# Attention, routing and two expert layers on one core: constants, masks and one-hots of the routing laid out anew

## Chip, core and metric

The kernel runs on 1 core of one Trainium2 chip. The metric is device time in microseconds (us). The engines are named as in the profile: PE (TensorE, matrix products; PEld its weight loads), DVE (VectorE), ACT (ScalarE), POOL (GpSimd) and SP (SyncE, which issues DMAs).

## What is computed

A linear attention with a decaying state (4 batches, 8 heads, 768 steps, head size 48), then a mixture of 8 experts with the best two per token, then a gated layer:

```python
for t in range(S):                                   # per batch and head
    state = alpha[:, :, t, :, None] * state + k_t (outer) v_t
    y[:, :, t] = q_t @ state
x = y rearranged to [3072, 384]
noisy = x @ w_gate + log1p(exp(x @ w_noise)) * noise
top2 = the two largest of 8;  w = softmax over the two
out[token] += w * (relu(x[token] @ w1[e]) @ w2[e])    # e over the two experts
result = ((out @ w_a) * (out @ w_b)) @ w_out
```

## The kernel before

The 3072 tokens are 24 tiles of 128. The attention runs one loop over the tiles (lines 756 to 783), in chunks of 128 steps, with the heads in four pairs. The order of instructions is written out by hand, and every engine works through its own queue in that order. For tile i the loop emits, in this order: loads; transposes of k of tile i+1 (L643); transposes of the output of tile i-1 (L724); `inter(i)`, the product of q with the carried state (L667); `sc_unit(i+1)`, the scores q k of the next tile on PE (L651) and their causal mask on DVE (L656); `prep(i+3)`; `intra(i)` (L675), which uses the masked scores; `gm_unit(i-1)`, the gate products (L736); `u_unit` and `s_unit` (L702, L717, L718), the new state; and a piece of weight preparation (L110 on ACT, L111 on POOL) in tiles 6 to 21.

`prep` works out the decays. DVE scans backward (L621, "scan D") into `Ds` and forward (L625, "scan A") into `At`; POOL multiplies k by D (L623), q by A (L626), and makes the decay of the state (L629). Both scans take a reset pattern from `inject`, which fills PSUM bank 7: a 3-element memset (L620) sets the backward scan's ones, a reciprocal (L624) the values that the forward scan needs.

The scores of the even and the odd heads lie in PSUM banks 2 and 3; each is masked by an instruction of its own (L656, twice per tile) into `pm0` and `pm1`.

Routing runs beside this in pieces: generators in `side`, of which `tick()` advances each by one step. `choose(s)` (lines 236 to 309) works on a sub-group of 4 or 5 tiles (`SUBS`): logits and noise to the two best experts, with the softplus on ACT and POOL. `route(g)` (lines 311 to 404) follows for each of the two groups of 14 and 10 tiles (`GROUPS`): it counts ranks by products with triangular matrices, and makes the list of expert 0's tokens out of one-hot matrices (`eq`, `bt`, `at`, lines 365 to 378) whose products (L384) scatter token numbers into a table. `lists(g)` (lines 406 to 450) does the same for the other experts, in sets of 4 or 5 tiles (L426, L432, products L447). Gathers by these lists (L479) bring tokens together for the experts.

While POOL is busy, the small tiles of the first four sub-groups and of the first group lie in PSUM bank 5 (`place`, lines 177 to 187), those of the last ones in SBUF. Bank 6 (`UG`) holds the state products (L702), the gate products and the list tables. Accesses of two engines to one bank are ordered one after the other.

The one-hot tiles are 16-bit with the position innermost (`[tile, 128]` or `[tile, 49]`); `lane` and `keys`, the constants that they are compared with, are 16-bit too, the values compared (`pf`, `kf`, `val`, `token`) are 32-bit and constant along the innermost axis.

From 152 us on PE runs the experts' products (L801 to L803) and, from about 580 us, the gated layer's.

Of the kernel before, what the change touches and what calls it, by code (L numbers as in the profile page):

```python
# [7 lines left out]
F32 = mybir.dt.float32  # L8
F32R = mybir.dt.float32r
F16 = mybir.dt.float16  # L10
# [9 lines left out]
NP = H // 2  # L20
# [3 lines left out]
E = 8  # L24
# [33 lines left out]
def moe_kernel(ctx: ExitStack, tc, qka, afirst, v, wgn, noise, w1, w2, w3, out):  # L58
# [10 lines left out]

    def bank(i):  # L70
        return tl(psum, [128, 512], F32, f"bank{i}")
# [131 lines left out]
    def route_consts():  # L203
        nc.sync.dma_start(wgn_t, wgn)
        nc.sync.dma_start(noise_t, noise)
        iota(e4096, [[4096, E]])
        iota(prio, [[-1, E]], base=E)
        iota(keys.rearrange("p (e j) -> p e j", e=E), [[32, E], [1, NJ]])
        iota(lane, [[1, 128]])
        iota(token, [[256, NT // 2], [1, 2]], base=-1024, channel=2)  # L210
# [25 lines left out]
    def choose(s):  # L236
# [10 lines left out]
        def scr(name, *shape):  # L247
            return scratch(name, (5, *shape), last)[:, :n]
# [7 lines left out]
        lg = scr("lg", E)  # L256
        z, az, ex, w, c, r, ln, mz, sp = (tmp(x) for x in ("z", "az", "ex", "w", "c", "r", "ln", "mz", "sp"))
# [53 lines left out]
    def route(g):  # L311
# [34 lines left out]
        pi, ki = (scr(x, I32) for x in ("pi", "ki"))  # L346
        pf, kf, val = (scr(x) for x in ("pf", "kf", "val"))
        ri = val.bitcast(I32)
# [12 lines left out]
        else:  # L361
# [3 lines left out]
        eq, bt = (tl(rt, [128, HOT, 2, WL], F16, x, bufs=2).rearrange("p a k w -> p (a k w)")[:, :n * NJ]  # L365
                  .rearrange("p (a w) -> p a w", a=n) for x in ("eqk", "bt"))
        nc.vector.tensor_tensor(val, oav[:, :, 0], token[:, i0:i0 + n], op=ALU.mult)
        nc.vector.tensor_tensor(eq, keys[:, None, :NJ].to_broadcast([128, n, NJ]),
                                kf[:, :, None].to_broadcast([128, n, NJ]), op=ALU.is_equal)
        nc.vector.tensor_tensor(bt, eq, val[:, :, None].to_broadcast([128, n, NJ]), op=ALU.mult)  # L370
        yield
        m = n if n <= 2 * HOT else n // 2
        ats = []
        for j0 in range(0, n, m):
            at = tl(rt, [128, HOT, 2, 128], F16, "at", bufs=2).rearrange("p a k w -> p (a k) w")[:, :m]
            nc.vector.tensor_tensor(at, lane[:, None, :].to_broadcast([128, m, 128]),
                                    pf[:, j0:j0 + m, None].to_broadcast([128, m, 128]), op=ALU.is_equal)
            ats.append(at)
            yield
# [3 lines left out]
        for j in range(n):  # L383
            nc.tensor.matmul(pl, ats[j // m][:, j % m], bt[:, j], start=j == 0, stop=j == n - 1)  # L384
# [20 lines left out]

    def lists(g):
# [4 lines left out]
                          for x, dt in (("ei", I32), ("ri", I32), ("rf", F32), ("e1", F32)))  # L411
# [7 lines left out]
        def make(s):  # L419
            j0, j1 = s  # L420
            m = j1 - j0
            at, eq, bt = (tl(rt, [128, HOT, 2, w_], F16, x, bufs=2)[:, :m]
                          for x, w_ in (("at", 128), ("eqk", WL), ("bt", WL)))
            for out_, src, val in ((at, lane, pf), (eq, keys[:, NJ:], kf)):
                w_ = src.shape[-1]
                nc.vector.tensor_tensor(out_.rearrange("p a k w -> p (a k) w"),  # L426
                                        src[:, None, :].to_broadcast([128, 2 * m, w_]),
                                        val[:, j0 - i0:j1 - i0].rearrange("p a k -> p (a k)")[:, :, None]
                                        .to_broadcast([128, 2 * m, w_]), op=ALU.is_equal)
                yield  # L430
            for k in range(2):
                nc.vector.tensor_tensor(bt[:, :, k], eq[:, :, k],  # L432
                                        token[:, j0:j1, None].to_broadcast([128, m, WL]), op=ALU.mult)
            hot[s] = m, at, bt

        yield from make(sets[0])
        for s, after in zip(sets, sets[1:] + [None]):
            if after:
                yield from make(after)
            else:  # L440
                for _ in range(LAG - 1):
                    yield
            m, at, bt = hot.pop(s)
            pl = spot(1, WL)
            for j in range(m):
                for k in range(2):
                    nc.tensor.matmul(pl, at[:, j, k], bt[:, j, k], start=j + k == 0, stop=j == m - 1 and k == 1)  # L447
            yield
            nc.vector.tensor_tensor((idx if s[1] == NT else lacc)[:, NJ:], pl, lacc[:, NJ:], op=ALU.add)
        yield  # L450

    def weights():

        ei, ri, rf = (tl(rt, [128, NT, 2], dt, x) for x, dt in (("ei", I32), ("ri", I32), ("rf", F32)))
# [114 lines left out]
    with ExitStack() as actx:  # L569
        big = actx.enter_context(tc.tile_pool(name="abig", bufs=1))  # L570
        work = actx.enter_context(tc.tile_pool(name="awork", bufs=2))
# [27 lines left out]
        nc.vector.memset(inject, 0.0)  # L599
        Ds = [tl(big, [128, 512], F32, f"D{i}") for i in range(2)]  # L600
# [12 lines left out]
        def prep(i):  # L613
# [6 lines left out]
            nc.vector.memset(inject[:, 128::128], 1.0)  # L620
            nc.vector.tensor_tensor_scan(Dt[:, :511][:, ::-1], t[:, 1025:1536][:, ::-1], inject[:, 1:][:, ::-1], 1.0,  # L621
# [25 lines left out]
        def sc_unit(i):  # L647
            pb = [bank(2), bank(3)]
            for p in range(NP):
                for h in range(2):  # L650
                    nc.tensor.matmul(pb[h][:, p * 128:p * 128 + 128], part(i, h, NP + p), part(i, h, p),  # L651
                                     start=True, stop=True)
            PM[i] = []
# [102 lines left out]
        for i in range(NT):  # L756
# [9 lines left out]
            if i + 1 < NT:  # L766
                sc_unit(i + 1)
            else:
                x_unit(0, 0, bank(2))
                x_unit(0, 1, bank(3))  # L770
# [19 lines left out]

    hpool = sctx.enter_context(tc.tile_pool(name="hpool", bufs=1))
# [490 lines left out]
```

## Time and profile before

| | |
|---|---|
| time, median of 3 runs | 1036.9 us (1036.23 to 1038.09) |
| profiled execution: its time | 1040.05 us |
| profiled execution: its span | 1038.30 us |
| mean granted TensorE clock | 0.982 |
| busy: PE, DVE, ACT, POOL | 1005.3, 563.1, 385.1, 414.6 us |

All times in the rows below count from the start of the span of the profiled execution. A row of the timeline gives start, duration, engine, line, operation, output and inputs, and in brackets how long the engine stood idle before it and what released it; "x2" is two instructions merged in one row. Rows of one line give the shortest, the median and the longest duration of its instructions in ns. L656 is line 656 of the kernel before. "bank" is a PSUM bank; other names are SBUF tiles unless the text says otherwise.

### The profile page before, as it was taken

The page shows a single profiled execution, that of the slowest core. Times are in us where ns is not written, and L with a number is a line of the kernel's source. Part 1 is how long each engine was busy: PE and PEld are TensorE (multiplying, and loading weights), DVE is VectorE, ACT ScalarE, POOL GpSimd, SP SyncE. Part 2 cuts the span into 40 slices and gives each one's busy share as a digit, 9 for nine tenths or more (in the row PEclk, how much of TensorE's full clock was granted, in tenths as well). Part 3 has the DMA queues.
Part 4 walks back from the last instruction along what each step waited for, and adds up shares of the span by engine and source line. Part 5 has one row for each costly group of instructions (what it writes and reads, how often), then busy time and mean ns, then how long its engine had stood idle before and what let it go on. Part 6 is the DMA issues. An engine that isn't in the chain of part 4 may idle for free.

```text
span 1038.3 us, 17572 instructions
## 1 busy us (share of the span) xinstructions
PE 1005.3 (97%) x6698; PEld 931.8 (90%) x6698; DVE 563.1 (54%) x983; ACT 385.1 (37%) x831; POOL 414.6 (40%) x443
## 2 busy tenths in 40 slices
PE   7999689999999999999999999999999999999997
PEld 5888679999999999999999888888888888888886
DVE  8998667576676776767764454232233332333221
ACT  2555331454444444545443344222222222222212
POOL 5687441475766676868673334020020020000000
PEclk9999679999999999999999999999999999999999
DMA  9787110657686886897856535131140140020000
GB/s 334 263 300 244 59 55 27 182 177 215 210 236 188 233 239 197 236 249 222 221 156 182 143 107 137 38 104 18 42 111 1 46 107 1 31 62 1 31 1 33
DMA packets 118850, 141.13 MB, mean 136 GB/s; under 512 B 66272, under 2 KB 102752, under 8 KB 118752
## 3 DMA queue, kind: packets, MB, share of 16 engines
q1 hardware_dynamic: 112224, 120.13, 38.6%
q0 software_dynamic: 6528, 19.67, 6.6%
q8 instruction: 64, 1.05, 0.4%
q14 instruction: 34, 0.28, 0.1%
HBM read 101.43 MB, written 38.34 MB: 135 GB/s over the span
## 4 chain that ended last, share of the span: by engine, by line
PE 79%; DVE 7%; issue 3%; DMA 2%; POOL 2%; ACT 1%; SPq 0%; POOLq 0%; DVEq 0%
PE bank L801 25%; PE bank L803 25%; PE bank L802 25%; DVE pm L656 1%; DVE D L621 1%; DVE A L625 1%; DMA row<-xd,idx 1%; POOL W L111 1%; PE bank L667 1%; PE bank L651 1%; DMA xt<-tb 1%; PE bank L487 0%; DMA raw<-xt 0%; DMA y<-o 0%; POOL row L479 0%
## 5 line engine op out<-in xcount | busy, mean ns | idle before, releaser
L1113 DVE TENSOR_TENSOR p<-bank,a 128x512 f32<-128x512 f32 x72 | 49.8, 691 | 253.2 <-PE bank L803 253.2
L111 POOL TENSOR_TENSOR W<-wst,W 128x384 fp32r<-128x384 f32 x136 | 147.9, 1097 | 88.7 <-ACT W L110 83.5
L801 PE MATMUL bank<-X,W 128*128 128x416 f32 (+4 forms) x474 | 168.6, 356 | 0.5 <-ACT X L489 0.4
L802 PE MATMUL bank<-X,W 128*128 128x416 f32 (+3 forms) x474 | 167.8, 354 | 0.0
L803 PE MATMUL bank<-X,W 128*128 128x416 f32 (+3 forms) x474 | 167.7, 354 | 0.0
L801 PE MATMUL bank<-HB,W 128*128 128x416 f32 (+4 forms) x474 | 167.5, 353 | 0.0
L803 PE MATMUL bank<-HB,W 128*128 128x416 f32 (+3 forms) x474 | 166.5, 351 | 0.0
L802 PE MATMUL bank<-HB,W 128*128 128x416 f32 (+3 forms) x474 | 166.5, 351 | 0.0
L975 POOL DMA_INDIRECT row<-y,row x48 | 47.0, 978 | 206.0 <-DVE row L983 170.4
L845 ACT ACTIVATE HB<-bank 128x416 fp32r<-128x416 f32 (+2 forms) x128 | 65.9, 517 | 109.7 <-PE bank L803 96.4
L1111 ACT ACTIVATE a<-bank 128x512 f32<-128x512 f32 x72 | 43.1, 599 | 167.9 <-PE bank L803 166.0
L1115 ACT ACTIVATE HB<-p 128x512 fp32r<-128x512 f32 x72 | 45.5, 632 | 156.8 <-DVE p L1113 152.5
L846 DVE SCALAR_TENSOR_TENSOR HB<-bank,HB 128x416 fp32r<-128x416 f32 (+2 forms) x128 | 72.7, 582 | 45.4 <-ACT HB L845 41.1
L801 PEld LDWEIGHTS bank<-X,W 128*128 128x128 f32 x474 | 89.7, 189 | 4.6 <-ACT X L489 0.6
L803 PEld LDWEIGHTS bank<-X,W 128*128 128x128 f32 x474 | 89.6, 189 | 4.1
L802 PEld LDWEIGHTS bank<-X,W 128*128 128x128 f32 x474 | 89.7, 189 | 3.6
L803 PEld LDWEIGHTS bank<-HB,W 128*128 128x128 f32 x474 | 89.0, 188 | 4.0
L801 PEld LDWEIGHTS bank<-HB,W 128*128 128x128 f32 x474 | 89.1, 188 | 3.6
L802 PEld LDWEIGHTS bank<-HB,W 128*128 128x128 f32 x474 | 89.0, 188 | 3.7
L1116 DVE TENSOR_TENSOR HB<-p,HB 128x512 fp32r<-128x512 f32 x72 | 49.8, 692 | 50.3 <-ACT HB L1115 50.3
L110 ACT ACTIVATE W<-wst 128x384 fp32r<-128x384 f32 x144 | 71.9, 515 | 10.3 <-DMA wst<-w 8.6
L479 POOL DMA_INDIRECT row<-xd,idx x56 | 58.9, 1052 | 39.8 <-DVE idx L388 23.1
(240 smaller groups left out, 1960.9 us busy)
## 6 DMA issues: line engine op xcount, KB each, us to landing
wst<-w SPq DMA_DIRECT2D x128, 192.0 KB
ring<-qka SPq DMA_DIRECT2D x22, 768.0 KB
wd<-w SPq DMA_DIRECT2D x36, 384.0 KB
y<-o SPq DMA_DIRECT2D x56, 156.0 KB
xt<-tb SPq DMA_DIRECT2D x11, 768.0 KB
raw<-xt SPq DMA_DIRECT2D x44, 192.0 KB
w3f<-u SPq DMA_DIRECT2D x36, 192.0 KB
wst<-w3f SPq DMA_DIRECT2D x36, 192.0 KB
```

What stands on the lines that cost most here:

```text
L110: nc.scalar.activation(h, raw, AF.Copy)
L111: eng.tensor_tensor(l, raw, h.bitcast(F32), op=ALU.subtract)
L479: nc.gpsimd.indirect_dma_start(out=t[:m], out_offset=None, in_=xd[:SPLIT * 128] if a else xd, in_offset=bass.IndirectOffsetOnAxis(ap=ix, a ...
L801: nc.tensor.matmul(ps[:, :m], ah, bh[:, :m], start=first, stop=False)
L802: nc.tensor.matmul(ps[:, :n], ah, bl[:, :n], start=False, stop=False)
L803: nc.tensor.matmul(ps[:, :n], al, bh[:, :n], start=False, stop=last)
L845: nc.scalar.activation(Hh[:, f, s], pu[:, :n], AF.Relu)
L846: nc.vector.scalar_tensor_tensor(Hl[:, f, s], pu[:, :n], 0.0, Hh[:, f, s].bitcast(F32), op0=ALU.max, op1=ALU.subtract)
L975: nc.gpsimd.indirect_dma_start(out=t, out_offset=None, in_=src, in_offset=bass.IndirectOffsetOnAxis(ap=row[:, i, k:k + 1], axis=0))
L1113: nc.vector.tensor_tensor(p, ps[1], a, op=ALU.mult)
L1115: nc.scalar.activation(h, p, AF.Copy)
L1116: nc.vector.tensor_tensor(l, p, h.bitcast(F32), op=ALU.subtract)
```

## The change

- The backward scan gets a constant `resets` in SBUF, written once by POOL; the memset of each tile goes. The forward scan keeps `inject` in PSUM.
- The two score banks become one tile of two banks, and one instruction of 1024 elements per partition masks both.
- `lg` of `choose`, the logits without noise, always lies in SBUF.
- `pf`, `kf`, `val` and `token` become 16-bit and lie in SBUF. The one-hot tiles are turned: the position is the outer axis, the tiles of a set are innermost, so that every operand runs along the innermost axis. `lane` and `keys` are written out ten times over for that. `bt` of a set is one instruction instead of two. PE reads each one-hot at a stride of the number of tiles in it.
- Tiles of `weights` get names of their own.

```diff
-    keys = tl(rt, [128, E * NJ], F16, "keys")
-    lane = tl(rt, [128, 128], F16, "lane")
-    token = tl(rt, [128, NT], F32, "token")
+    keys = tl(rt, [128, E * NJ, 2 * HOT], F16, "keys")
+    lane = tl(rt, [128, 128, 2 * HOT], F16, "lane")
+    token = tl(rt, [128, NT, 2], F16, "token")
...
-        lg = scr("lg", E)
-        z, az, ex, w, c, r, ln, mz, sp = (tmp(x) for x in ("z", "az", "ex", "w", "c", "r", "ln", "mz", "sp"))
+        z, az, ex, w, c, r, ln, mz, sp, lg = (tmp(x) for x in ("z", "az", "ex", "w", "c", "r", "ln", "mz", "sp", "lg"))
...
-        pi, ki = (scr(x, I32) for x in ("pi", "ki"))
-        pf, kf, val = (scr(x) for x in ("pf", "kf", "val"))
-        ri = val.bitcast(I32)
+        pi, ki, ri = (scr(x, I32) for x in ("pi", "ki", "ri"))
+        pf, kf, val = (tmp(x, 1, F16) for x in ("pf", "kf", "val"))
...
+            at = hot_tile("at", 128, m)
+            nc.vector.tensor_tensor(at, lane[:, :, :m], pf[:, None, j0:j0 + m].to_broadcast([128, 128, m]),
+                                    op=ALU.is_equal)
...
-            nc.tensor.matmul(pl, ats[j // m][:, j % m], bt[:, j], start=j == 0, stop=j == n - 1)
+            nc.tensor.matmul(pl, ats[j // m][:, :, j % m], bts[j // m][:, :, j % m], start=j == 0, stop=j == n - 1)
...
+    def hot_tile(name, w, m):
+
+        size = {"at": 128, "eqk": WL, "bt": WL}[name]
+        t = tl(rt, [128, size * 2 * HOT], F16, name, bufs=2)
+        return t[:, :w * m].rearrange("p (w t) -> p w t", t=m)
...
-            for k in range(2):
-                nc.vector.tensor_tensor(bt[:, :, k], eq[:, :, k],
-                                        token[:, j0:j1, None].to_broadcast([128, m, WL]), op=ALU.mult)
+            nc.vector.tensor_tensor(bt, eq, token[:, j0:j1].rearrange("p a k -> p (a k)")[:, None, :]
+                                    .to_broadcast([128, WL, 2 * m]), op=ALU.mult)
...
+        resets = tl(big, [128, 512], F32, "resets")
+        nc.gpsimd.memset(resets, 0.0)
+        nc.gpsimd.memset(resets[:, ::128], 1.0)
...
-            nc.vector.memset(inject[:, 128::128], 1.0)
-            nc.vector.tensor_tensor_scan(Dt[:, :511][:, ::-1], t[:, 1025:1536][:, ::-1], inject[:, 1:][:, ::-1], 1.0,
+            nc.vector.tensor_tensor_scan(Dt[:, :511][:, ::-1], t[:, 1025:1536][:, ::-1], resets[:, 1:][:, ::-1], 1.0,
                                          op0=ALU.mult, op1=ALU.add)
...
-            pb = [bank(2), bank(3)]
+            pb = scores()
...
-            for h in range(2):
-                m = tl(work, [128, NP, 128], F32, f"pm{h}")
-                nc.vector.tensor_tensor(m, pb[h].rearrange("p (a t) -> p a t", a=NP),
-                                        causal[:, None, :].to_broadcast([128, NP, 128]), op=ALU.mult)
-                PM[i].append(m)
+            m = tl(work, [128, 2, NP, 128], F32, "pm")
+            nc.vector.tensor_tensor(m.rearrange("p h a t -> p (h a) t"), pb.rearrange("p h (a t) -> p (h a) t", a=NP),
+                                    causal[:, None, :].to_broadcast([128, 2 * NP, 128]), op=ALU.mult)
```

## Rows read from the trace of the kernel before

**Rows 1.** The page's chain that ended last, by engine, shares of the span.

```profile
PE 79%; DVE 7%; issue 3%; DMA 2%; POOL 2%; ACT 1%; SPq 0%; POOLq 0%; DVEq 0%
```

**Rows 2.** Stretches: length, busy us (instructions) of PE, PEld, DVE, ACT, POOL; clock, DMA.

```profile
52.00:84.00 32.00, 29.95 (x583) 27.41 (x582) 29.99 (x71) 16.87 (x45) 28.29 (x38) 1.00 0.82 291
84.00:107.00 23.00, 20.88 (x363) 19.07 (x363) 19.36 (x43) 12.46 (x35) 17.70 (x25) 0.93 0.69 246
186.00:1038.00 852.00, 843.56 (x4353) 786.12 (x4352) 415.22 (x645) 312.82 (x642) 309.65 (x293) 1.00 0.45 126
```

**Rows 3.** Timeline, DVE: the mask of a tile without routing work.

```profile
29.55 1.29 DVE L656 TENSOR_TENSOR pm<-bank,causal 128x512 f32<-128x512 f32 x2 [0.32 <-PE bank L651]
```

**Rows 4.** Timeline, DVE and POOL: a tile with a part of `choose`.

```profile
48.91 0.51 POOL L718 TENSOR_TENSOR sc<-ss,aend 128x192 f32<-128x192 f32 x1
...
49.39 1.22 DVE L621 TENSOR_TENSOR_SCAN D<-ring,bank 128x511 f32<-128x511 f32 x1
...
50.29 1.00 POOL L111 TENSOR_TENSOR W<-wst,W 128x384 fp32r<-128x384 f32 x1
...
51.60 0.27 POOL L280 TENSOR_TENSOR r_sp<-r_sp,noise 128x40 f32<-128x40 f32 x1
51.83 1.27 POOL L623 TENSOR_TENSOR ring<-ring,D 128x512 f32<-128x512 f32 x1
...
52.00 0.18 DVE L284 TENSOR_TENSOR bank<-r_sp,bank 128x40 f32<-128x40 f32 x1
...
53.42 1.28 DVE L656 TENSOR_TENSOR pm<-bank,causal 128x512 f32<-128x512 f32 x2
...
54.80 1.22 DVE L621 TENSOR_TENSOR_SCAN D<-ring,bank 128x511 f32<-128x511 f32 x1
```

**Rows 5.** One-hots and the nearest faster DVE line (ns); timeline: `bt`, and who waits.

```profile
L426 DVE TENSOR_TENSOR at<-lane,rf x5: 1214/1486/1493, 143.7 to 175.7; 128x1280 f16<-128x1280 f16 x4, 128x1024 f16<-128x1024 f16 x1
...
L942 DVE TENSOR_SCALAR u<-wd x36: 340/350/1656, 196.1 to 534.7; 128x384 int32<-128x384 int32 x36
...
147.12 0.72 DVE L432 TENSOR_TENSOR bt<-eqk,token 128x245 f16<-128x245 f16 x2
...
151.32 0.83 PE L736 MATMUL bank<-wgn,gx 128*64 128x16 f32 x12 [2.27 <-DVE lacc L449]
```

**Rows 6.** Lines (ns: shortest, median, longest) and timeline: DVE and POOL on SBUF together.

```profile
L952 DVE SCALAR_TENSOR_TENSOR u<-wd,rf x36: 501/1360/1883, 201.4 to 544.1; 128x384 int32<-128x384 int32 x36
...
222.85 1.61 DVE L952 SCALAR_TENSOR_TENSOR u<-wd,rf 128x384 int32<-128x384 int32 x1
223.00 1.03 POOL L111 TENSOR_TENSOR W<-wst,W 128x384 fp32r<-128x384 f32 x1
...
145.46 0.66 DVE L426 TENSOR_TENSOR eqk<-keys,e 128x490 f16<-128x490 f16 x1
145.62 0.63 POOL L306 TENSOR_TENSOR oa<-oh,oh 128x40 f32<-128x40 f32 x1 [3.38 <-DVE oh L298]
...
L626 POOL TENSOR_TENSOR ring<-ring,A x23: 1263/1276/1289, 11.0 to 131.8; 128x512 f32<-128x512 f32 x23
```

**Rows 7.** The same stretches for line L621 (scan D) alone: busy us (instructions).

```profile
52.00:84.00 32.00, 7.31 (x6) 1.00 0.82 291
84.00:107.00 23.00, 5.18 (x5) 0.93 0.69 246
```

**Rows 8.** Timeline, ACT and PE: sub-group 3's logits beside the first group's routing.

```profile
122.00 0.19 ACT L259 ACTIVATE bank<-bank 128x40 f32<-128x40 f32 x1 [3.26 <-DVE bt L370]
...
122.24 0.88 PE L702 MATMUL bank<-v,kn 128*48 128x48 f32 x16 [4.30 <-ACT bank L259]
```

**Rows 9.** Timeline, PE's weight loads: strided, contiguous, and of one-hots as they are.

```profile
148.10 0.42 PEld L487 LDWEIGHTS bank<-ident,row 128*128 128x128 f32 x3
...
148.44 0.37 PEld L724 LDWEIGHTS bank<-ident,x 128*128 128x128 f32 x3
...
154.17 0.51 PEld L447 LDWEIGHTS <-at 128*128 128x128 f16 x10 [0.31 <-issue]
```

More of the change, by code (lines that the diff above doesn't have):

```diff
@@ L68, in moe_kernel @@
     psum = ctx.enter_context(tc.tile_pool(name="psum", bufs=1, space=PSUM))
+    late = []
     def bank(i):
-        return tl(psum, [128, 512], F32, f"bank{i}")
+        return tl(late[0] if i in (2, 3) else psum, [128, 512], F32, f"bank{i}")
     xd = tc.dram_tile([N, DM], F32, name="xd")
@@ L207, in route_consts @@
         iota(prio, [[-1, E]], base=E)
-        iota(keys.rearrange("p (e j) -> p e j", e=E), [[32, E], [1, NJ]])
-        iota(lane, [[1, 128]])
-        iota(token, [[256, NT // 2], [1, 2]], base=-1024, channel=2)
+        iota(keys.rearrange("p (e j) t -> p e j t", e=E), [[32, E], [1, NJ], [0, 2 * HOT]])
+        iota(lane, [[1, 128], [0, 2 * HOT]])
+        iota(token, [[256, NT // 2], [1, 2], [0, 2]], base=-1024, channel=2)
         nc.gpsimd.memset(lacc, 1024.0)
@@ L364, in route @@
         yield
[L365 to L370, printed above, removed]
+        m = n if n <= 2 * HOT else n // 2
+        nc.vector.tensor_tensor(val, oav[:, :, 0], token[:, i0:i0 + n, 0], op=ALU.mult)
+        bts, ats = [], []
+        for j0 in range(0, n, m):
+            eq, bt = (hot_tile(x, NJ, m) for x in ("eqk", "bt"))
+            nc.vector.tensor_tensor(eq, keys[:, :NJ, :m], kf[:, None, j0:j0 + m].to_broadcast([128, NJ, m]),
+                                    op=ALU.is_equal)
+            nc.vector.tensor_tensor(bt, eq, val[:, None, j0:j0 + m].to_broadcast([128, NJ, m]), op=ALU.mult)
+            bts.append(bt)
         yield
-        m = n if n <= 2 * HOT else n // 2
-        ats = []
         for j0 in range(0, n, m):
-            at = tl(rt, [128, HOT, 2, 128], F16, "at", bufs=2).rearrange("p a k w -> p (a k) w")[:, :m]
-            nc.vector.tensor_tensor(at, lane[:, None, :].to_broadcast([128, m, 128]),
-                                    pf[:, j0:j0 + m, None].to_broadcast([128, m, 128]), op=ALU.is_equal)
+            at = hot_tile("at", 128, m)
+            nc.vector.tensor_tensor(at, lane[:, :, :m], pf[:, None, j0:j0 + m].to_broadcast([128, 128, m]),
+                                    op=ALU.is_equal)
             ats.append(at)
@@ L421, in make @@
             m = j1 - j0
-            at, eq, bt = (tl(rt, [128, HOT, 2, w_], F16, x, bufs=2)[:, :m]
-                          for x, w_ in (("at", 128), ("eqk", WL), ("bt", WL)))
+            at, eq, bt = (hot_tile(x, w_, 2 * m) for x, w_ in (("at", 128), ("eqk", WL), ("bt", WL)))
             for out_, src, val in ((at, lane, pf), (eq, keys[:, NJ:], kf)):
[L425 to L429, printed above, removed]
+                w_ = src.shape[1]
+                nc.vector.tensor_tensor(out_, src[:, :, :2 * m],
+                                        val[:, j0 - i0:j1 - i0].rearrange("p a k -> p (a k)")[:, None, :]
+                                        .to_broadcast([128, w_, 2 * m]), op=ALU.is_equal)
                 yield
-            for k in range(2):
-                nc.vector.tensor_tensor(bt[:, :, k], eq[:, :, k],
-                                        token[:, j0:j1, None].to_broadcast([128, m, WL]), op=ALU.mult)
+            nc.vector.tensor_tensor(bt, eq, token[:, j0:j1].rearrange("p a k -> p (a k)")[:, None, :]
+                                    .to_broadcast([128, WL, 2 * m]), op=ALU.mult)
             hot[s] = m, at, bt
@@ L446, in lists @@
                 for k in range(2):
-                    nc.tensor.matmul(pl, at[:, j, k], bt[:, j, k], start=j + k == 0, stop=j == m - 1 and k == 1)
+                    nc.tensor.matmul(pl, at[:, :, 2 * j + k], bt[:, :, 2 * j + k], start=j + k == 0,
+                                     stop=j == m - 1 and k == 1)
             yield
@@ L570, in moe_kernel, with scores @@
         big = actx.enter_context(tc.tile_pool(name="abig", bufs=1))
+        pss = actx.enter_context(tc.tile_pool(name="pss", bufs=1, space=PSUM))
+        def scores():
+            return tl(pss, [128, 2, 512], F32, "scores")
         work = actx.enter_context(tc.tile_pool(name="awork", bufs=2))
@@ L768, in moe_kernel @@
             else:
-                x_unit(0, 0, bank(2))
-                x_unit(0, 1, bank(3))
+                pb = scores()
+                x_unit(0, 0, pb[:, 0])
+                x_unit(0, 1, pb[:, 1])
             if i + 3 < NT:
@@ L788, in moe_kernel @@
         tick()
+    late.append(ctx.enter_context(tc.tile_pool(name="psum2", bufs=1, space=PSUM)))
     hpool = sctx.enter_context(tc.tile_pool(name="hpool", bufs=1))
```

8 lines of the change are left out of this document (4 added, 4 removed).

## Prediction, made before the changed kernel was run

> **What bounds the kernel now.** First the chain that ended last: 79% of it is PE [rows 1]. Then the table of stretches [rows 2]: from 186 us to the end PE is busy 843.56 of 852.00 us at a mean granted clock of 1.00, in products that the change doesn't touch, so whatever is won or lost before that should reach the end unchanged. The question is the attention stage. In 52 to 84 us PE has 29.95 of 32.00, DVE 29.99 and POOL 28.29 busy: three engines, none with much room. The timeline says who waits for whom. In the quiet tiles around 30 us DVE's mask waits 0.32 us for PE's scores [rows 3]: there PE sets the pace. From about 49 us on, when POOL also splits weights (L111) and does a part of `choose`, DVE goes from the mask to scan D without a gap [rows 4].
>
> **Part 1, resets in SBUF, one mask.** Removed: the 3-element memset and one of two masks per tile. A mask pair takes 1.28 us [rows 4]. The two lengths of the one-hot row give the price of an element, (1486 - 1214) / 256 = 1.06 ns, and a fixed part of 1486 - 1280 x 1.0625 = 126 ns [rows 5]; one mask of 1024 elements is then 1.21 us, 0.07 less. From the end of the mask (53.42 + 1.28 = 54.70) to scan D are 0.10 us [rows 4]; nearly all of that is the memset. So 0.15 us of DVE time a tile, 3.6 us over 24 if DVE set every pace. From 24 to 49 us it doesn't [rows 3]; there the saving only lengthens the wait for PE. I take -0.4 us, for the first three tiles (ends 0 and -3.6). Added: POOL writes `resets` and ten times larger `keys` and `lane`, at the very start, while its first work for the tiles comes later; nothing.
>
> Moved: scan D's second operand from PSUM to SBUF, so that scan D has two SBUF inputs. What that means is seen away from the scan. L952 has two SBUF inputs; it takes 0.50 us at its shortest, 1.36 in the median, 1.88 at most. At 222.85 it takes 1.61 us, and ends (224.46) after POOL's L111 (to 224.03) with about the length that it needs alone. The other way round POOL's L306 takes 0.63 us for 40 elements (L718, with 192, needs 0.51 [rows 4]) while DVE makes `eqk` (to 146.12) from two SBUF inputs: it ends at 146.25. Beside the scans as they are, with one operand in PSUM, POOL's L626 never varies: 1263 to 1289 ns over 23 [rows 6]. So a DVE instruction with two SBUF inputs and a POOL instruction exclude each other here, whole instruction by whole instruction. No row shows it for a scan.
>
> The Trainium skill has this as a rule (SBUF — State Buffer, Who interferes with whom): a Vector instruction with two SBUF inputs contends with a GpSimd instruction that reads SBUF, and whoever is first blocks the other for the whole instruction. By it, scan D joins in; by the rows alone a scan could still be an exception. The page measures no scan.
>
> What it costs, from both sides. Floor: in 52 to 84 us POOL's 28.29 plus six scans, 7.31 [rows 7], are 35.6 us for a stretch of 32.0: +3.6. In 84 to 107, 17.70 + 5.18 = 22.9 of 23.0: 0. Ceiling: each of the eleven scans costs its whole 1.22: +13.4. Between them, by walking the tile at 49 us [rows 4]. DVE asks for scan D 0.15 early, at 49.25; POOL's L718 holds until 49.42; D runs to 50.64. All that POOL does next (`choose`'s products, L111, to L280 at 51.60 + 0.27) moves by 1.22 us and ends at 53.1. L623 follows it at once, as it does now (51.83), until 54.3. Behind L280 DVE waits with L284; with `lg` in SBUF this too has two SBUF inputs, and comes after L623: 54.3 instead of 52.00. DVE's queue is in order, so the rest of `choose` and the mask (53.42) move by 2.3 us. The next scan D then meets L111 again: L623 to 54.3, L626 1.28, L718 0.51, L111 1.00, so not before 57.1 against 54.80. With a further wait of some 0.2 us in the second tile of the pair that is +2.5 us for one `choose`. Three lie between 49 and 107 us (sub-groups 0 to 2): +7.5 us. I take that, since the walk follows the queues; plain tiles I leave at nothing, as DVE has some slack there.
>
> **Part 2, logits in SBUF.** `lg` of sub-group 3 now lies in PSUM bank 5, where DVE works on `route(0)`: ACT's L259 waits 3.26 us, until L370 is done, and PE's L702, which needs bank 6 free of ACT, waits 4.30 us for L259 [rows 8]. With `lg` in SBUF, L259 runs at 122.00 - 3.26 = 118.74, L702 at about 119.0, and PE's next scores come as much earlier. Next late is DVE, with `route(0)`'s one-hots; they end before those scores. -3.1 us (ends -3.3, and 0 if another wait takes its place).
>
> **Part 3, one-hots.** Now 1280 elements take 1.49 us, `eqk` 0.66, the two halves of `bt` 0.72 together [rows 5, 6]. Afterwards all operands are 16-bit and run along the innermost axis. No row shows a two-operand DVE instruction above one element per 1.06 ns; the nearest faster one is L942, one operand, 384 in 350 ns: (350 - 126) / 384 = 0.58 ns an element [rows 5]. At that rate 1280 take 0.87, `eqk` and an undivided `bt` 0.41 each: 2.87 becomes 1.69, 1.2 us per set. Unchanged rate: about 0.1. I take the faster one. On the path lie the two sets before L736, which waits 2.27 us for L449 behind them [rows 5]. Of 2.4 us I count -1.5, since in front of L449 DVE also has to finish X of the third tile, which waits for ACT (ends 0 and -2.27). Later sets run beside PE's products: 0.
>
> The Trainium skill (VectorE: DVE Perf Modes, the perf-mode tier table) gives `tensor_tensor` on 16-bit SBUF operands twice the rate, and no more. An estimate by it, 1280 x 1.06 / 2 + 126 = 0.80 us, would make this term hardly different; no run yet shows it.
>
> PE now reads the one-hots at a stride of up to 10 elements. The trace has a strided load, every third column of `row` (L487), three in 0.42 us, against 0.37 for contiguous `x` (L724): 17 ns more each [rows 9]. 58 products after 141 us, where PE is the bound: +1.0 us. Ends: 0, and 58 times the difference between 0.37 / 3 = 123 and 51 ns (ten present loads in 0.51, L447): +4.2. Pool and bank naming, the split `ei`, `ri`, `rf`: nothing, as no wait names them.
>
> **Sum.** -0.4 + 7.5 - 3.1 - 1.5 + 1.0 = +3.5 us. The profiled execution took 1040.05 us (span 1038.30) and would take 1043.55; it stands 3.15 over the median, so the forecast is 1036.9 + 3.5 = 1040.4 us.
>
> **Rivals.** A, faster: scan D doesn't exclude POOL. Then the ten tiles of 52 to 107 us in which DVE sets the pace win 0.15 each: -0.4 - 1.5 - 3.1 - 1.5 + 1.0 = -5.5, 1031.4 us. For it: no row has such a scan, and the scan takes over 2 ns an element (1.22 us for 511), so it needn't read in every cycle. Against: [rows 6]. It decides if POOL's L111 keeps running under scan D.
> B, no change: they exclude each other, but POOL's lag is taken up by the three tiles that `prep` is ahead, and only the floor is left: -0.4 + 3.6 - 3.1 - 1.5 + 1.0 = -0.4, 1036.5 us. Against: L718 stands behind the lag in POOL's queue, and ACT, then PE, wait for it within a tile.
> C, slower still: PE's longer waits lower its clock. In 84 to 107 us the mean grant is 0.93 [rows 2]; of the two levels, 1.2 and 2.4 GHz, that is 14% or 3.2 us at the lower one, 1.6 us of work lost. Once more per `choose`: +4.8, 1045.2 us.
> That the change doesn't do what it says, one-hots at the old rate, gives 1041.9, inside the forecast's range.
>
> **How the numbers follow.** Forecast 0.40, A 0.27, B 0.23, C 0.10. About 0.2%, 2.1 us, is what a measurement can tell from no change. Faster: A and 0.04 of B, 0.31. Same: 0.15 of B and 0.09 of the forecast's low side, 0.24. Slower: the rest, 0.45. The range from 1030.5 to 1045.5 takes in A and most of C and leaves out the tails of both; the forecast's own is 1037.5 to 1043.5.
>
> **What would show it.** In the changed profile: scan D longer than 1.22 us in many of its 24, or POOL's L111, L718 and `choose` products stretched under it; L284 waiting behind L623; tile periods from 49 to 107 us up by some 0.7 on the mean; no wait of L259 on L370 and none of L702 over 1.5 us near 119 us; the 1280-element one-hot near 0.8 to 0.9 us; strided loads a little longer. POOL and scan D unmoved beside each other would overturn the main term and give A.

## The result, and the profile after

The changed kernel takes 1049.8 us in the median against 1036.9 before: ratio 1.0111, 95% interval 1.0077 to 1.0145. Two later groups of executions of the same kernel gave 1.0085 (1.0066 to 1.0104) and 1.0077 (1.0064 to 1.0091). It is slower, as forecast, but by 11.5, 8.8 and 8.0 us by these ratios (12.9 by the two medians of the first group) where 3.5 were forecast. The profiled execution took 1051.33 us (span 1049.6). In what follows a ratio is turned into us with the median of before that was timed beside it; a thousandth is 1.04 us.

The page's chain that ended last, by engine, answers to [rows 1]; the stretches (length, busy us and instructions of PE, PEld, DVE, ACT, POOL; clock, DMA) answer to [rows 2]. The stretch from 20 to 36 us is added; its line for the kernel before stands at the end.

```profile
PE 87%; DVE 6%; POOL 2%; issue 2%; DMA 1%; ACT 1%; SPq 0%; POOLq 0%; DVEq 0%; ACTq 0%
```

```profile
20.00:36.00 16.00, 14.14 (x236) 13.05 (x230) 10.38 (x14) 4.99 (x12) 9.60 (x12) 0.79 0.51 177
52.00:84.00 32.00, 28.65 (x506) 26.07 (x502) 25.34 (x41) 14.35 (x39) 27.43 (x36) 0.89 0.68 239
...
84.00:107.00 23.00, 21.05 (x289) 19.80 (x286) 17.28 (x32) 11.40 (x32) 17.64 (x21) 0.73 0.58 211
...
186.00:1038.00 852.00, 850.08 (x4402) 792.09 (x4401) 414.87 (x652) 311.61 (x641) 311.59 (x296) 1.00 0.44 126
```

```profile
20.00:36.00 16.00, 15.18 (x290) 14.14 (x291) 14.42 (x26) 7.12 (x17) 11.15 (x14) 1.00 0.74 261
```

Up to 107 us PE is nearly as busy as before but does less: 236 instructions in 20 to 36 instead of 290, at a mean granted clock of 0.79 instead of 1.00, and 289 in 84 to 107 instead of 363, at 0.73 instead of 0.93. The timeline of all engines at 22 us shows how that begins; the second fence has the same steps of the kernel before.

```profile
21.91 1.21 DVE L633 TENSOR_TENSOR_SCAN D<-ring,resets 128x511 f32<-128x511 f32 x1
21.93 1.19 POOL L641 TENSOR_TENSOR aend<-af,D 128x4 f32<-128x4 f32 x1
...
23.08 0.50 POOL L728 TENSOR_TENSOR sc<-ss,aend 128x192 f32<-128x192 f32 x1
...
23.61 0.73 ACT L701 ACTIVATE Sbd<-sc 64x192 f32<-64x192 f32 x2 [2.37 <-POOL sc L728]
...
24.40 1.13 PE L677 MATMUL bank<-Sbd,ring 128*128 128x96 f32 x8 [1.60 <-ACT Sbd L701]
...
26.70 1.95 PE L685 MATMUL bank<-v,pm 128*64 128x48 f32 x32
```

```profile
21.16 0.20 POOL L629 TENSOR_TENSOR aend<-af,D 128x4 f32<-128x4 f32 x1
...
22.65 1.13 PE L667 MATMUL bank<-Sbd,ring 128*128 128x96 f32 x8 [0.62 <-ACT Sbd L691]
...
24.80 1.14 PE L675 MATMUL bank<-v,pm 128*64 128x48 f32 x32
```

Scan D has begun 0.02 us before POOL's four-element product, and this takes 1.19 us instead of 0.20. Behind it sc, ACT's Sbd and PE are late; PE waits 1.60 us instead of 0.62, and two steps later its 32 products take 1.95 us, not 1.14. That is the lower of the two clocks: the granted clock of 26 to 33 us is 0.52. In a tile with a part of `choose` (timeline; the lines of [rows 4]):

```profile
57.40 1.27 POOL L635 TENSOR_TENSOR ring<-ring,D 128x512 f32<-128x512 f32 x1
...
57.47 1.26 DVE L285 TENSOR_TENSOR bank<-r_sp,r_lg 128x40 f32<-128x40 f32 x1 [0.84 <-POOL r_sp L281]
...
61.10 1.45 DVE L633 TENSOR_TENSOR_SCAN D<-ring,resets 128x511 f32<-128x511 f32 x1
```

L285 has 40 elements and took 0.18 us before [rows 4, its L284]. It also waits out POOL's product, as the prediction's walk had it. The stall of [rows 8] is gone: in PE's timeline the wait is 0.94 us, not 4.30.

```profile
132.10 0.88 PE L712 MATMUL bank<-v,kn 128*48 128x48 f32 x16 [0.94 <-ACT r_lg L260]
```

The lines of the one-hots (ns: shortest, median, longest) answer to [rows 5, 9]. The timeline behind them has the first two row tiles, gathered tokens that PE transposes for the experts (`x_unit`).

```profile
L451 PEld LDWEIGHTS <-at x48: 138/143/167, 157.8 to 191.3; 128*128 128x128 f16 x48
...
L432 DVE TENSOR_TENSOR at<-lane,rf x5: 682/819/826, 152.9 to 184.8; 128x1280 f16<-128x1280 f16 x4, 128x1024 f16<-128x1024 f16 x1
```

```profile
154.49 0.54 DVE L495 TENSOR_TENSOR X<-scores,X 128x384 fp32r<-128x384 f32 x1
...
155.09 0.62 PE L492 MATMUL scores<-ident,row 128*128 128x128 f32 x3 [2.39 <-DVE X L495]
...
160.97 0.83 PE L746 MATMUL bank<-wgn,gx 128*64 128x16 f32 x12 [0.74 <-DVE lacc L454]
```

DVE's 1280 elements take 0.82 us instead of 1.49, and the wait behind them 0.74 instead of 2.27. But PE waits 2.39 us ahead of the second row tile's transposes (L492), until DVE's X of the first is done (L495): both row tiles now lie in the two halves of one PSUM tile. Run e12 below shows that this is the cause.

Where the time comes and goes is seen best at fixed points of each trace (us from the span's start): the starts of some of the 24 scans D (D5 is tile 5's), of the first expert product (prod3's first matmul) and of the 60th such product. Each kernel but the first and the last two is the one before with a single part of the change.

| Kernel | D5 | D10 | D21 | D23 | first product | 60th |
|---|---|---|---|---|---|---|
| before | 26.29 | 49.39 | 106.69 | 129.01 | 152.09 | 191.69 |
| resets in SBUF (e2) | 28.19 | 51.24 | 110.76 | 132.35 | 155.40 | 194.98 |
| logits in SBUF (e3) | 27.09 | 50.18 | 109.97 | 127.91 | 150.99 | 190.56 |
| one mask (e4) | 26.87 | 49.96 | 105.26 | 127.41 | 152.03 | 193.32 |
| one-hots (e5) | 26.40 | 49.49 | 105.22 | 125.78 | 147.31 | 188.91 |
| changed, another execution (e6) | 28.18 | 52.93 | 114.89 | 132.58 | 156.03 | 197.61 |
| changed | 27.95 | 53.94 | 120.63 | 138.31 | 161.72 | 203.30 |

The profiled execution of before has itself a stretch at the lower clock (0.93 in 84 to 107 us, [rows 2]), which e4's and e5's don't have (1.00): their 1.4 us at D21 are that, not a gain. The traces don't start alike either: scan D4, ahead of all the waits told here, begins at 21.45 us before, at 22.39 in e2 and at 20.95 in e6. So it is differences between two columns that are read below, not single times.

### The profile page after: what moved, and what is told of

It reads as the page before. It is cut to its first block, busy times and chain, and to the rows that moved or that the text cites. A ratio compares the mean times of both kernels' runs of the same rounds, so it can differ in the third digit from the quotient of the medians.

```text
span 1049.6 us, 17505 instructions
## 1 busy us (share of the span) xinstructions
PE 1017.7 (97%) x6698; PEld 942.8 (90%) x6698; DVE 551.5 (53%) x932; ACT 385.0 (37%) x831; POOL 427.1 (41%) x445
## 4 chain that ended last, share of the span: by engine, by line
PE 87%; DVE 6%; POOL 2%; issue 2%; DMA 1%; ACT 1%; SPq 0%; POOLq 0%; DVEq 0%; ACTq 0%
PE bank L813 26%; PE bank L815 26%; PE bank L814 26%; PE scores L663 2%; PE bank L685 1%; PE bank L677 1%; DVE pm L666 1%; DVE D L633 1%; DVE A L637 1%; PE bank L655 1%; DMA row<-xd,idx 1%; PE bank L624 1%; PE bank L712 1%; PE bank L492 1%; POOL row L987 1%
```

## The experiments

The edits are shortened: `scan(...)` stands for the call in full, a line in words for several lines of code, and lines without a change are left out.

**Each part alone.** e2_resets:

```
+resets = tl(big, [128, 512], F32, "resets")
+nc.gpsimd.memset(resets, 0.0)
+nc.gpsimd.memset(resets[:, ::128], 1.0)
-nc.vector.memset(inject[:, 128::128], 1.0)
-scan(Dt, t[:, 1025:1536], inject[:, 1:])
+scan(Dt, t[:, 1025:1536], resets[:, 1:])
```

> The kernel before with one part of the change: scan D's resets in an SBUF tile, the 3-element memset gone; masks, logits and one-hots as before. Theory (the clock theory): scan D and POOL's instructions exclude each other already in the tiles of 20 to 36 us, where POOL's aend and sc then come late, PE waits for Sbd and its granted clock falls to 1.2 GHz for some ten us; nearly the whole loss of the change is here, so +10 to +15 us over before (1047 to 1052), with a granted clock below 1.00 somewhere in 16 to 40 us. Rival 1 (the prediction's own term): exclusion costs only in the tiles with a choose, +6 to +8 us, clock 1.00 until 50 us. Rival 2 (the loss comes from the other parts): between -3 and +1 us.

Measured: 1.0048 (1.0035 to 1.0061), +5.0 us (3.6 to 6.3): far below the 10 to 15 of the clock theory, and nearest to the prediction's own 6 to 8. The lines (ns: shortest, median, longest) and one of PE's timeline:

```profile
L623 DVE TENSOR_TENSOR_SCAN D<-ring,resets x24: 1210/1224/1770, 4.1 to 132.4; 128x511 f32<-128x511 f32 x24
...
L631 POOL TENSOR_TENSOR aend<-af,D x20: 201/204/1128, 12.4 to 136.4; 128x4 f32<-128x4 f32 x20
...
L720 POOL TENSOR_TENSOR sc<-ss,aend x16: 503/507/1417, 22.5 to 143.7; 128x192 f32<-128x192 f32 x16
```

```profile
24.73 1.13 PE L669 MATMUL bank<-Sbd,ring 128*128 128x96 f32 x8 [1.52 <-ACT Sbd L693]
```

The same late Sbd in the same tile, but here the clock stayed at 1.00 from 20 to 107 us. From D10 to D21 the scans take 59.52 us, against 55.73 in e5, which has no low clock there either: the exclusion costs 3.8 us between 49 and 107 us, and about one (D4 to D5, +0.96) in the early tile, where the prediction had nothing. The 3.8 are close to the prediction's floor of 3.6, but by luck: they stand at the tiles with a part of `choose` (D10 to D11 6.17 us against 5.42 in e5, D15 to D16 6.56 against 5.42, D19 to D20 6.17 against 5.23) and in the tile after each, as the walk has it, and 1.6 of them fall between D16 and D21, for which the floor had 0.

e3_lg:

```
-lg = scr("lg", E)
+lg = tmp("lg")
```

> The kernel before with one part of the change: the logits lg in SBUF; all else as before. Theory and prediction: the waits of ACT's copy of the logits and of PE's next scores near 119 us go, -3 to -4 us. Rival: the wait is replaced by another one within the same tiles, between -1 and +0.5 us.

Measured: 0.9993 (0.9982 to 1.0004), -0.7 us: the rival's number, but not its reason. From D22 to D23 the kernel needs 8.63 us, 3.5 less than before: the stall was won. It was paid for in `choose` of the sub-groups 0 to 2 (timeline, DVE and POOL):

```profile
52.61 1.27 POOL L622 TENSOR_TENSOR ring<-ring,D 128x512 f32<-128x512 f32 x1
52.79 1.15 DVE L283 TENSOR_TENSOR bank<-r_sp,r_lg 128x40 f32<-128x40 f32 x1
```

nl's two inputs now both lie in SBUF, and 40 elements wait until POOL's product is over. After this D11 is 1.0 us later than D10 was; the same in the next sub-group (1.0) and the third (0.7). That is 2.7 us; from D21 to D22 it gained 0.9.

e4_mask:

```
-pb = [bank(2), bank(3)]
+pb = scores()        # one PSUM tile of two banks
-two masks of 128x512
+one mask of 128x1024
-x_unit(0, 0, bank(2)); x_unit(0, 1, bank(3))
+x_unit(0, 0, pb[:, 0]); x_unit(0, 1, pb[:, 1])
```

> The kernel before with one part of the change: one PSUM tile for both score banks, one mask for both, and the first two transposed row tiles in the halves of that tile. Theory: one mask instead of two makes no difference that shows in the attention tiles (within 1 us), but the second row tile's transposes wait for DVE's work on the first, as they share a tile, up to 2.4 us near 144 us; +0.5 to +2.5 us in all. Rival 1 (the prediction): nothing or -0.4 us. Rival 2: a mask over both banks holds up PE's next scores in every tile, +5 us or more.

Measured: 1.0036 (1.0024 to 1.0048), +3.7 us (2.5 to 5.0), more than the theory allowed. In the tiles nothing is lost (the table, up to D23). The timeline has the wait that the changed kernel has too (DVE and PE):

```profile
144.52 0.55 DVE L492 TENSOR_TENSOR X<-scores,X 128x384 fp32r<-128x384 f32 x1
145.12 0.91 PE L489 MATMUL scores<-ident,row 128*128 128x128 f32 x3 [3.37 <-DVE X L492]
```

PE waits 3.4 us, D23 to the first product grows from 23.08 to 24.62, and the first 60 products take 41.29 us instead of 39.60; from the 9th to the 17th they need 8.3 us instead of 5.8 (starts 6.51 and 14.81 after the first, 7.27 and 13.08 before). Between these PE waits 1.57 us for DVE's `xc` (at 161.85), and the matmuls behind that take 0.52 us each instead of 0.33, the lower clock again.

e5_onehot (the one-hot hunks of the change alone):

> The kernel before with one part of the change: the one-hots all 16-bit with tiles innermost (and the tenfold keys and lane constants written at the start). Theory: DVE's one-hot of 1280 elements takes about 0.8 us instead of 1.49 and wins 1 to 1.5 us ahead of the first expert products, while 58 products with strided weight loads cost 0.05 to 0.07 us each, +3 to +4 us: +1.5 to +3 us in all. Rival 1 (the prediction): -0.5 us. Rival 2: POOL's long constants at the start delay the first tile and that carries on, another +1 us or more at the first scores.

Measured: 1.0006 (0.9991 to 1.0021), +0.6 us (-0.9 to 2.2); the rival's -0.5 and the lower end of the theory's 1.5 to 3 both lie inside, so the time decides nothing. D23 to the first product shrinks by 1.55 (23.08 to 21.53), the first 60 products grow by 2.0 (39.60 to 41.60); the long constants at the start shift D10 by 0.10. The stall of [rows 8] shrinks too, from 4.30 to 3.23 us: `pf`, `kf` and `val` no longer lie in bank 5, and ACT waits there until L362 only, not L370. With the logits in SBUF that gain has nothing left to win. The twelve executions fall into two groups by their mean clock: seven at 0.986 or 0.987 take 1035.0 to 1038.0 us, five at 0.978 to 0.982 take 1039.8 to 1043.3.

The four parts alone add up to 5.0 - 0.7 + 3.7 + 0.6 = +8.6 us. The second and third group of the whole change (+8.8, +8.0) agree with that, within the intervals of some 2 us; the first has 3 us more. But equal sums don't show equal terms, as the clock shows next.

**The clock.** e6_again and e15_third are the changed kernel as it is.

> The changed kernel as it is, once more, beside the others of this group. Theory: the three stretches at a granted clock of 0.50 that its first profile shows (26 to 33, 74 to 81 and 95 to 108 us) belong to the kernel and not to one execution; they come in most executions, 1048 to 1052 us, and an execution that goes without one or two of them takes about 3 us less for each. Rival: they were a chance of that chip or that hour, and here it takes 1040 to 1044 us, the sum of the parts' own losses (resets +4, mask +3, logits -1, one-hots 0).

> The changed kernel as it is, a third group of executions. Theory: the waits of PE are the same in each execution and the granted clock behind them isn't, so the median may fall anywhere between the 1045.6 and the 1049.8 us of the first two groups, and the executions with the lowest mean clock are the longest. Rival: the first group was of another kind, and it stays at 1044 to 1046.

Measured: 1045.6 us (1044.0 to 1048.0) and 1044.5 us (1042.6 to 1048.5). e6's median lies between its theory (1048 to 1052) and its rival (1040 to 1044), 1.6 us above the latter, and e15's is its rival's: there the theory was wrong in that the median fell below both earlier ones. Its other half holds: the longest execution of each group has the lowest mean clock (0.978, 0.978), and in the first group the four long ones have 0.976 to 0.979 and the one of 1042.5 has 0.987. In the first trace PE waited 1.60 us for Sbd at 24.40, 1.79 for it at 73.22 and 1.43 for r_lg at 95.13, and behind each of the three the clock fell: 0.52 in 26 to 33 us, 0.51 in 74 to 80, 0.50 in 96 to 108. In e6's trace the same three waits are there, 1.60, 1.79 and 1.42 us; only the first was followed by a low clock (0.58 in 23 to 29 us). Its timeline and stretches for the other two:

```profile
72.21 1.13 PE L677 MATMUL bank<-Sbd,ring 128*128 128x96 f32 x8 [1.79 <-ACT Sbd L701]
```

```profile
72.00:78.00 6.00, 5.79 (x107) 5.36 (x107) 3.94 (x5) 4.93 (x17) 4.79 (x6) 1.00 0.33 112
93.00:99.00 6.00, 5.78 (x113) 5.46 (x114) 5.06 (x6) 4.02 (x16) 5.29 (x7) 1.00 0.07 28
```

e15's trace, an execution of 1048.5 us, has the second and third wait once more (1.79 us at 72.22, 1.43 at 94.28), and behind both the clock fell (0.52 in 74 to 80 us, 0.50 in 94 to 107):

```profile
94.28 0.89 PE L712 MATMUL bank<-v,kn 128*48 128x48 f32 x16 [1.43 <-ACT r_lg L260]
```

```profile
84.00:107.00 23.00, 20.96 (x283) 19.50 (x282) 16.43 (x32) 10.53 (x30) 17.49 (x24) 0.71 0.58 206
```

So equal waits at equal places end differently from execution to execution. D21 is 5.7 us earlier in e6 than in the first trace (1.0 of it ahead of D4, 4.7 from D10 on), and the first product too; e15's first product, at 161.31, is as late as the first trace's.

e8_fill puts work in the waits:

```
+def fill(t):
+    for _ in range(3):
+        nc.tensor.matmul(t[:, :256], ones, junk[:, :256], start=True, stop=True)
 PY[i] = bank(4)
+if i in (2, 11):
+    fill(PY[i])
 pu = UG
+if i == 15:
+    fill(bank(4))
```

> The changed kernel, and at the three places where its PE waited 1.4 to 1.8 us before the clock fell, three matmuls of 256 columns of ones that nothing reads, 1.3 us at full clock, issued in the wait: ahead of the state products of the tiles 2 and 11 and of tile 15's update. Theory: it is these waits that lower the clock; with PE at work in them the granted clock stays at 1.00 from 20 to 36 us and from 68 to 84 us, and better than 0.73 from 84 to 107 us, and the time falls by 4 to 9 us although nothing else is removed. Rival: the clock falls there for another reason or comes down at the next wait; then the time is as in the changed kernel or up to 4 us more.

Measured: 1.0057 (1.0039 to 1.0075), 1043.3 us; beside the unfilled kernel of the same group (1.0085) 2.9 us less, where 4 to 9 less were expected. Its stretches:

```profile
20.00:36.00 16.00, 15.43 (x278) 14.12 (x277) 13.25 (x17) 6.58 (x15) 11.65 (x14) 1.00 0.60 205
...
84.00:107.00 23.00, 22.08 (x388) 19.82 (x385) 20.72 (x36) 12.40 (x35) 19.69 (x26) 1.00 0.65 238
```

The clock is 1.00 until 107 us, and D4 to D10 takes 28.93 us where e6, with its one low stretch, needs 31.98. The intervals of the two runs overlap, so the gain in time alone doesn't prove it, nor does one trace: at the first place e2's clock stayed at 1.00 behind an unfilled wait of 1.52 us, at the other two e6's did. That the clock falls behind PE's waits is seen in three traces and supported by this run, not shown by it; what decides in one execution and not in the next stays open. Without any low clock before 107 us, the kernel still loses 62.0 - 55.7 = 6.3 us from D10 to D21 against e5 (51.30 to 113.29, 49.49 to 105.22); e6 needs 62.0 there too.

**Undoing the largest part.** e1_noreset is the changed kernel with inject and its memset back; e7_noreset_apart has besides x_unit(0, 1) without the shared tile.

> The changed kernel with scan D's resets put back into the PSUM tile of before, with the 3-element memset; one mask, logits in SBUF and one-hots stay. Theory: without the exclusion of scan D and POOL the waits of PE for POOL's sc and aend, and the three stretches at 0.50 behind them, are gone: 1037 to 1041 us, some 9 to 12 less than the changed kernel. Rival: resets are worth only the +4 us that they cost alone, 1045 to 1047 us.

> The kernel of the run before this one (resets back in PSUM), and the second row tile's transposes in a PSUM bank of their own, not in the second half of the tile that the first row tile's work reads. Theory: the wait of 2.4 to 3.4 us for DVE's X of the first row tile goes, 1 to 3 us less than with the shared tile. Rival: DVE's X of both row tiles is what the next step waits for anyway, within 0.5 us of the run with the shared tile.

Measured: e1 1.0020 (1.0005 to 1.0035), +2.1 us; beside 1.0085 of the whole change that is 6.7 us less, between the theory's 9 and the rival's 4; the median, 1039.3 us, lies in the theory's 1037 to 1041. D10 to D21 takes 57.98 us, 4.0 less than in e8. e7: 1.0012 (0.9996 to 1.0027), 0.8 less than e1, inconclusive as a time. Its trace has D23 to the first product at 21.45 us against 24.01 in e1, but also a late start (below), which hides it in the span. So the single part was tried again.

**The shared tile.** e12_mask_apart, from e4:

```
-x_unit(0, 1, pb[:, 1])
+x_unit(0, 1)
```

> The kernel before with one PSUM tile for both score banks and one mask, as in the earlier run of that part (+3.7 us), but with the second row tile's transposes in a bank of their own. Theory: the whole loss of that part is the wait of 3.4 us for DVE's X of the first row tile and the lower clock behind it: here between -1 and +1.2 us. Rival: the shared tile of the scores or the one mask costs in the attention tiles, +2.5 us or more as before.

Measured: 0.9997 (0.9985 to 1.0009), -0.3 us, against +3.7 with the shared tile. The two row tiles are transposed in one go (timeline, PE), and D23 to the first product is 23.00:

```profile
141.25 0.52 PE L489 MATMUL scores<-ident,row 128*128 128x128 f32 x3
141.61 0.50 PE L489 MATMUL bank<-ident,row 128*128 128x128 f32 x3
```

So one line of the change cost 4 us as far as this part alone goes. Some of it is clock: e4's eleven executions have a mean clock of 0.981 in the median, e12's twelve 0.986, and e12's products keep 0.34 us behind the `xc` wait, which is 0.94 us there.

**The exclusion by itself.** e11_both_scans, from before:

```
-inject = bank(7)
+inject = tl(big, [128, 512], F32, "inject")
```

> The kernel before with the tile of the scans' second operands, inject, in SBUF and not in PSUM: scan A too then has two SBUF inputs; the memsets stay. Theory (a scan with two SBUF inputs and a POOL instruction exclude each other): POOL's product of K, which runs beside scan A now, waits for it or scan A waits for POOL, about 1.2 us in most of the 24 tiles: +20 to +45 us. Rival (the loss with resets in SBUF comes from something else than exclusion, their memset or the order of the start): at most the +5 us of that run.

Measured: 1.0256 (1.0239 to 1.0273), +26.5 us. Scan A, 1219 to 1221 ns in all 24 tiles of before, becomes (lines; timeline, POOL and DVE):

```profile
L625 DVE TENSOR_TENSOR_SCAN A<-ring,inject x24: 1225/2185/2236, 5.7 to 153.8; 128x512 f32<-128x512 f32 x24
```

```profile
30.89 1.27 POOL L623 TENSOR_TENSOR ring<-ring,D 128x512 f32<-128x512 f32 x1 [1.16 <-DVE D L621]
31.06 2.18 DVE L625 TENSOR_TENSOR_SCAN A<-ring,inject 128x512 f32<-128x512 f32 x1
```

POOL's product ends at 32.16, the scan 1.08 us later, a little less than its own length. It waited, it wasn't slowed. The Trainium skill (SBUF — State Buffer, Who interferes with whom) has Vector instructions with two SBUF inputs contend with GpSimd's reads, and calls the contention an exclusive lock. It names no scan, and this is the number for one.

**Logits where they pay.** e9_lg_late, from before:

```
-lg = scr("lg", E)
+lg = scr("lg", E) if s < 3 else tl(rt, [128, 5, E], F32, "r_lg", bufs=2)[:, :n]
```

> The kernel before with the logits in SBUF for the sub-groups 3 and 4 alone; sub-groups 0 to 2 keep them in PSUM. Theory: with all logits in SBUF the stall near 119 us (4.4 us of scan 23's start) was won, but the addition that makes nl, with both inputs in SBUF, waited about 1.0 us for POOL in each of the sub-groups 0 to 2; without these three waits the gain is 2.5 to 4.5 us (1033 to 1035). Rival: the logits are worth no more than the 0.7 us of the run with all of them, within 1 us of before.

Measured: 0.9969 (0.9959 to 0.9979), -3.2 us, 1033.3. nl is short again in the sub-groups 0 to 2 (lines), and PE's wait near 117 us is 0.94 us (timeline):

```profile
L284 DVE TENSOR_TENSOR bank<-r_sp,bank x3: 176/181/183, 52.2 to 97.3; 128x40 f32<-128x40 f32 x2, 128x32 f32<-128x32 f32 x1
```

```profile
116.95 0.89 PE L702 MATMUL bank<-v,kn 128*48 128x48 f32 x16 [0.94 <-ACT r_lg L259]
```

**The one-hots.** e10_lg_late_onehot is e9 with the change's one-hots; e13_half_rows is e9 with 16-bit operands and the tiles outermost as before; e14_half_rows_mask is e13 with the one mask, row tiles apart as in e12. The core of e13:

```
-token = tl(rt, [128, NT], F32, "token")
+token = tl(rt, [128, NT], F16, "token")
-pf, kf, val = (scr(x) for x in ("pf", "kf", "val"))
+pf, kf, val = (tmp(x, 1, F16) for x in ("pf", "kf", "val"))
```

> The kernel of the run before this one, with the one-hots all 16-bit and tiles innermost as in the change. Theory: DVE's faster one-hots win 1.5 us between scan 23 and the first expert product and about as much ahead of it, and the strided weight loads lose 2.0 us among the first 60 products: within 1.5 us of the run without them. Rival: the strided loads outweigh the gain, over 1.5 us slower than without.

> The kernel before with the logits of sub-groups 3 and 4 in SBUF and all operands of the one-hots 16-bit, but the tiles outermost as before: PE reads its weights without a stride, and the value that is compared or multiplied is repeated along the innermost axis. Theory: the 2.0 us that the turned one-hots lost among the first 60 products were the strided weight loads; here they are not lost (the 40 products from the 21st to the 60th within 0.3 us of before's 24.4). Whether DVE keeps its doubled rate without the turn isn't known: if it does (1280 elements near 0.8 us), 1031 to 1033 us; if not (1.4 us), 1032.5 to 1034.5, as without the one-hots. Rival: the loss among the products stays, so it has another cause than the stride.

> The kernel of the run before this one with one mask over one PSUM tile of both score banks, the second row tile's transposes in a bank of their own. Theory: within 1 us of the run before this one, since the one mask saves 0.15 us of DVE in a tile and PE or POOL sets the pace in most; at best 1 us faster. Rival: up to 2 us slower, since the mask of the first bank can't begin before the products of the second are done.

Measured: e10 0.9965 (0.9952 to 0.9978), e13 0.9971 (0.9960 to 0.9982), both like e9: in neither form do the one-hots show a gain in time. e14 0.9954 (0.9941 to 0.9967), 1032.0 us, the fastest kernel here, 4.8 us (3.4 to 6.1) under before; against e13 that is 1.7 us less where 1 at best was expected, and the intervals overlap. What e13's lines show (ns):

```profile
L446 PEld LDWEIGHTS <-at x48: 95/98/147, 140.2 to 174.0; 128*128 128x128 f16 x48
...
L425 DVE TENSOR_TENSOR at<-lane,rf x5: 1214/1485/1493, 137.9 to 169.9; 128x1280 f16<-128x1280 f16 x4, 128x1024 f16<-128x1024 f16 x1
```

With all operands 16-bit but one of them repeated along the innermost axis DVE is as slow as before (1485 ns; 819 when turned). The weight loads are back at 98 ns from 143, and the 60th product comes 39.60 us after the first, as in before; in e10 it is 41.55. So the stride costs the 2.0 us: the turn that makes DVE faster makes PE slower.

## Why the prediction was off, step by step

- **"A DVE instruction with two SBUF inputs and a POOL instruction exclude each other", and scan D too**: right (e2, e11). Rival A falls. Rival B falls with the 6.3 us of e8: the lag wasn't taken up.
- **The walk, +2.5 for one `choose`, +7.5 for three**: right in mechanism, and somewhat large in size (6.3). It counted scan D and nl together; where no low clock disturbs (e8) the two cost 6.3 us from D10 to D21. In the two parts alone they are 3.8 (e2) and 1.0 + 1.0 + 0.7 (e3).
- **"Plain tiles I leave at nothing, as DVE has some slack there"**: wrong by about 1 us. The one who had no slack was POOL's aend and sc, then PE (the 1.5 to 1.6 us before tile 2's state products).
- **Logits, -3.1**: right for the stall (-3.5 from D22 to D23). The part alone is worth -0.7, since nl's waits belong to it; the prediction had booked these under Part 1. Together, -0.4 + 7.5 - 3.1 = +4.0 was forecast for resets and logits, and 5.0 - 0.7 = 4.3 measured. That these are so near is partly luck: the walk was 1.2 too large, the early tile 1.0 too small.
- **One-hots, -1.5 on DVE**: right (-1.55 from D23 to the first product), and the 0.87 us for 1280 elements is 0.82. **Strided loads, +1.0**: mis-sized, +2.0 measured, inside the bounds of 0 and 4.2 given there. The row it was taken from, `row` at every third column, was not like a step of ten 16-bit elements: 45 ns more for one load, not 17. The long constants cost nothing, as forecast.
- **"Pool and bank naming, the split ei, ri, rf: nothing, as no wait names them"**: this is the step that failed, for all executions: it put at nothing a term that measured +3.7 us. No wait named the banks because the two row tiles lay in two of them; in one tile the second's transposes wait for DVE's work on the first, 3.4 us in e4 and 2.39 in the changed kernel. Alone that is 3.7 us (e4), and with the row tiles apart nothing (e12); inside the change it is 1.9 us to the first product (23.45 in e6 against 21.53 in e5) or 2.6 (e1 against e7), and the times of e1 and e7 don't tell it. The change's full diff had it, in lines that the excerpt leaves out (`x_unit(0, 0, pb[:, 0])`, `x_unit(0, 1, pb[:, 1])`); the step looked for a wait in the trace of before instead of asking which instructions share a tile afterwards.
- **Rival C, PE's clock**: the second step that failed, and the larger one in the first group. The sum left the clock out and gave it to a rival with a chance of 0.10 and 1.6 us per `choose`. In e6 it fell once, at tile 2, far from any `choose`: 3.1 us (D4 to D10 28.93 in e8, 31.98 in e6). The first trace has that too (32.03) and two falls more, 4.7 us from D10 to D21. That rival C's 1045.2 is close to the later groups is luck: its 4.8 us were to be three falls at `choose`.

Stretch by stretch, e6's trace against before comes to some +8 us where +3.5 were forecast: `choose` +6.3 (against e5, which has no low clock), D21 to D23 -4.6 with the stall gone (17.69 against 22.32), one-hots and shared tile together +0.4 (23.45 against 23.08), strided loads +2.0, tile 2 +1.0 by exclusion and +3.1 by the clock. So the terms that the forecast had at nothing or too small are the clock 3.1, the shared tile 1.9, the early tile 1.0 and the strided loads 1.0; `choose` and the stall came out 2.7 better than forecast. That the four parts alone also add up to +8.6, near the later groups' 1045.6 and 1044.5, is partly luck: e2's trace has no low clock at tile 2, and e4's 3.7 holds some at another place. What the first group has beyond that, to 1049.8, goes with the low clock of four of its five executions; why those had it more often than the later groups isn't known.

## What to carry to other kernels

When operands move from PSUM to SBUF, count for each DVE instruction how many SBUF inputs it has afterwards, and which POOL instruction it meets: a short one on the way to PE (four elements, 1.2 us) costs as much as a long one. When two buffers become one tile, list who writes and who reads each half, since the halves now wait for each other. And take a change apart before judging it: of these four parts one was worth 3 us if done in two of its five places, one cost 4 us by a single line, and the whole lost 8 or more.

## What the runs showed of the hardware

The clock behind equal waits, and the rate of DVE with a repeated 16-bit operand, are told above. For the latter the Trainium skill (VectorE: DVE Perf Modes, What auto-detection actually checks) wants every tensor 16-bit with a step of one for this faster mode; the 1485 and 819 ns agree. One thing more wasn't expected: in some executions PE's first tiles run at about half speed although the granted clock of the stretch reads 1.00. In e15 (timeline, PE, and its stretch) the 16 products of scores take 2.08 us, against 1.16 in e6, the same kernel, at the same place (10.33), and D2 starts at 16.03 instead of 13.05. e7 has the same 2.08, at 12.38, and D2 at 16.10.

```profile
12.50 2.08 PE L663 MATMUL scores<-ring 48*128 48x128 f32 x16
```

```profile
12.00:14.00 2.00, 2.00 (x26) 1.91 (x24) 0.00 (x0) 0.00 (x0) 0.20 (x2) 1.00 1.01 424
```

So the first 20 us of two traces may differ by 3 us for no reason in the kernels, and the matmuls' own durations tell it where the clock's column doesn't.
